# Row sums by VectorE transposes and a gate applied on the copy out of PSUM, in a fused linear-attention and FFN block

## Chip, cores and metric

The kernel runs on one core of one Trainium2 chip. The metric is device time in microseconds; the time before is the median of three runs. The profiles show one execution. Engines: PE is TensorE, DVE is VectorE, ACT is ScalarE, POOL is GpSimd, SP is the queue that issues nearly all DMAs.

## The reference

One block of a conditioned transformer, S = 2048 tokens, D = 1024, 32 heads of 32, FFN width 3584, all in bf16:

```python
mod = (silu(c) @ w_mod).reshape(1, 6, 1, -1)         # c: (1, 1024), w_mod: (1024, 6144)
sa, ca, ga, sb, cb, gb = mod[:, 0], ...
h = layernorm(x) * (1 + ca) + sa
q, k, v = heads(h @ wqkv)
phi = lambda t: where(t > 0, t + 1, exp(t)) + 1e-6
kv = einsum('bhsd,bhse->bhde', phi(k), v);  z = phi(k).sum(over s)
num = phi(q) @ kv;  den = phi(q) . z + 1e-6
x = x + ga * ((num / den) @ wo)
h = layernorm(x) * (1 + cb) + sb
x = x + gb * ((gelu(h @ w_gate) * (h @ w_up)) @ w_down)
```

## The kernel before

Every instruction is recorded by hand with what it reads and writes; semaphores follow from that. PE and SP run in the recorded order. For the stretch from the last products of k to the first output-projection products, a planner (`reorder`, with a table of costs by name) orders DVE, ACT and POOL anew by due times.

The stages, with their place in the profile: layer norm and k of the first 512 tokens (to 31 us); q and k of the rest, with phi on ACT and DVE (to 127 us); the stage that the change touches (127 to 204 us); the rest of the output projection with the second layer norm beside it (to some 250 us); the FFN's gate and up products (to 602 us); the down products (to the end).

The stage from 127 us has 24 tiles of M = phi(k)^T x, eight head groups times three column tiles (k = 0, 1, 2), each of 16 matmuls (`m_tile`, L934) into PSUM banks 0 to 3 in turn. ACT copies each to SBUF (`mb`, L939). When a group's three tiles are there, a DMA transpose on SP brings M into the form `mtb` (`m_t`). Tiles 0 to 11 are groups 0 to 3, tiles 12 to 15 the first tiles of groups 4 to 7, and 16 to 23 the other two of each. A table `HOOK` puts other work behind certain tiles:

- `kv`: `kv_prod` multiplies the transposed M of a group with the weights of v (L952, bank 4); DVE masks the diagonal blocks into `kvt` (L956).
- `w`: `w2_pair` multiplies `kvt` with the group's rows of wo (L1235, banks 6 and 7); ACT copies the pair to `W2` (L1237). Before, wo has been multiplied by the gate ga ahead of that by eight DVE instructions (`wofold`, L1241).
- `den`: phi(q) times z for half of the tokens (L1262, 32 matmuls); DVE adds 1e-6, takes the reciprocal and casts it to `RDH` (L1267 to L1269), and a DMA stores it to DRAM. `rb` loads it back spread over partitions, and `pq_scale` (L1296) multiplies phi(q) by it. z comes from `z32` (L1229), which needs a column of each group's first tile.
- `ga`, `modp`, `gbr`: the modulation rows that are needed along the free axis (ga, then sb and cb, then gb).

Those rows are eight pieces of 512 columns. DVE accumulates each over the eight row blocks of w_mod (`macc`, L855, L858, L833, L835), one 128x512 instruction at a time, so 128 partial sums per column are left. To add them, ACT writes a bf16 part (`mhi`, L864, L842) and DVE the rest (`mlo`, L868, L843), and `mod_rows` multiplies both by a matrix of ones on PE (L879). ACT copies the result out (L886), SP stores it to the DRAM row `scr_row`, and loads bring it back: `gab` and `gbb` spread over all partitions, `sbT` and `cbT` as columns.

Afterwards `wo_mm` (L1304) multiplies the scaled phi(q) with `W2`, and DVE adds the result to x (L1313, L1317). The first three chunks of tokens are interleaved with the last W2 pairs.

Of the kernel before, what the change touches and what calls it, by code (L numbers as in the profile page):

```python
# [7 lines left out]
ACTF = mybir.ActivationFunctionType  # L8
ALU = mybir.AluOpType

P = 128
# [8 lines left out]
HPG = 4  # L20
# [169 lines left out]
class Sched:  # L190
# [41 lines left out]
    def dma(self, stream, fn, rd=(), wr=(), deps=(), note="", overwrite_ok=False):  # L232
# [6 lines left out]
        if prev is not None:  # L239
# [12 lines left out]
               "nm": (0.074, 0.085), "hmod": (0.25, 0.085), "macc": (0.66, 0.085), "mlo": (0.6, 0.085), "kvt": (0.21, 0.085), "z": (0.34, 0.085),  # L252
               "dene": (0.335, 0.085), "rden": (1.67, 0.085), "pqs": (0.62, 0.085), "wofold": (1.13, 0.085), "x": (1.14, 0.085), "ssum": (1.15, 0.085), "tsum": (1.15, 0.085), "padd": (0.62, 0.085), "yT": (0.62, 0.085)},
# [96 lines left out]
def bass_adaLN_cond__linear_attn_block__geglu_ffn__prompt_kernel(  # L350
# [18 lines left out]
    with ExitStack() as es:  # L369
# [53 lines left out]
        MROW = [at(f"mrow{i}", [P, 512], f32, OFF_ROW + i * 2048) for i in range(2)]  # L423
        MROW0 = at("mrowa", [P, 256], f32, XHO[2])
        WMG = [at(f"wmg{i}", [P, 4, 512], bf16, HBO[3] + i * 4096) for i in range(2)]
        MRG = at("mrg", [P, 256], f32, OFF_TMP + 4096)
        HLG = at("hlg", [P, 2, 2, 512], bf16, OFF_TMP)
        GAC = at("gacc", [P, 512], f32, OFF_TMP + 4096)
        ACC = [at(f"acc{i}", [P, 512], f32, OFF_ROW + i * 2048) for i in range(2)]
        HLO = OFF_WS + 16384  # L430
        HL = at("hl", [P, 4, 2, 512], bf16, HLO)
# [7 lines left out]
        for name, shape, dty, sz in [  # L439
            ("ident", [P, P], bf16, 256), ("bmask", [P, P], bf16, 256), ("bm32", [P, NG, NH], bf16, 512),   # L440
            ("z32", [P, NG, NH], bf16, 512), ("rdc", [P, SGW // 2], f32, 1024), ("rdh", [P, SGW // 2], bf16, 512),
            ("ones", [P, 32], bf16, 64), ("silf", [P, NDC], f32, 64),
            ("c8", [NDC, P], bf16, 256), ("cT", [P, NDC], f32, 64), ("chalf", [P, NDC], f32, 64),
            ("thc", [P, NDC], f32, 64), ("siluT", [P, NDC], bf16, 64), ("modt", [P, 16], f32, 64), ("add4", [P, 4], f32, 64),
            ("sbT", [P, NDC], f32, 64), ("cb1T", [P, NDC], f32, 64),
            ("cbT", [P, NDC], f32, 64), ("zcols", [P, NG], f32, 64), ("neghalf", [P, 1], f32, 64),
            ("st", [P, NCH, 12], f32, NCH * 48), ("mv", [P, NCH, 2], f32, NCH * 8),
            ("rs", [P, NCH], f32, 64), ("nm", [P, NCH], f32, 64), ("ve", [P, NCH], f32, 64),
        ]:
# [7 lines left out]
        ONES, SILF, C8, CT, CHALF, THC, SILUT = (_small[k] for k in ("ones", "silf", "c8", "cT", "chalf", "thc", "siluT"))  # L457
# [78 lines left out]

        def r_hl(k, h0, h1):
            return [(HLO + (2 * (k % 4) + h0) * 1024, HLO + (2 * (k % 4) + h1) * 1024, "hl")]

# [130 lines left out]
        sch.op(V, lambda e: e.memset(ONES[:, :], 1.0), wr=r_sm("ones"))  # L670
# [155 lines left out]
        def r_hlg(j, h):  # L826
            return [(OFF_TMP + (2 * j + h) * 1024, OFF_TMP + (2 * j + h + 1) * 1024, "hlg")]

# [11 lines left out]
        def gb_hilo(j):  # L840
            acc, rng = GA_[j]
            sch.op(A, lambda e: e.activation(HLG[:, j, 0, :], acc[:, :], ACTF.Copy), rd=rng, wr=r_hlg(j, 0), note=f"mhi{6 + j}")  # L842
            sch.op(V, lambda e: e.tensor_tensor(HLG[:, j, 1, :], acc[:, :], HLG[:, j, 0, :], ALU.subtract), rd=rng + r_hlg(j, 0), wr=r_hlg(j, 1), note=f"mlo{6 + j}")  # L843

        o_gb = [None]

        def gb_rows():
            mod_rows(((0, 2, 5, lambda j, h: (HLG[:, j, h, :], r_hlg(j, h))),))
            o_gb[0] = mod_store(2, 5, MRG, [(OFF_TMP + 4096, OFF_TMP + 5120, "mrg")], 2)

# [11 lines left out]
        def mod_hi(k):  # L862
            rng = r_2k(OFF_ROW + k % 2 * 2048, f"acc{k % 2}")
            sch.op(A, lambda e: e.activation(HL[:, k % 4, 0, :], ACC[k % 2][:, :], ACTF.Copy), rd=rng, wr=r_hl(k, 0, 1), note=f"mhi{k}")  # L864

        def mod_lo(k):
            rng = r_2k(OFF_ROW + k % 2 * 2048, f"acc{k % 2}")
            sch.op(V, lambda e: e.tensor_tensor(HL[:, k % 4, 1, :], ACC[k % 2][:, :], HL[:, k % 4, 0, :], ALU.subtract),  # L868
                   rd=rng + r_hl(k, 0, 1), wr=r_hl(k, 1, 2), note=f"mlo{k}")

        def mod_rows(parts):
            for k0, n, bank, src in parts:
                o = None
                w = n * P
                for h in range(2):
                    for j in range(4):
                        ap, rng = src(k0 + j * n // 4, h)
                        ap = ap[:, j * w % 512:j * w % 512 + w]
                        o = sch.op(T, lambda e, h=h, j=j, ap=ap, bank=bank, w=w: e.matmul(  # L879
                            ps_all[32 * j:32 * (j + 1), bank * 512:bank * 512 + w], ONES[:, :], ap, start=(h == 0), stop=(h == 1)),  # L880
                            rd=rng + r_sm("ones"), pwr=(pr(bank) if h == j == 0 else ()), note=f"modr{k0}.{h}.{j}")
                pset_writer(bank, o)

        def mod_store(n, bank, dst, rng, row):
            w = n * P
            sch.op(A, lambda e: e.activation(dst[:, 0:w], ps_all[:, bank * 512:bank * 512 + w], ACTF.Copy),  # L886
                   prd=pr(bank), wr=rng, note=f"mrow{row}")
            return sch.dma(Q, lambda e: e.dma_start(scr_row[row, 0:n, :].rearrange("a (h b) -> (a h) b", b=w), dst[0:128:32, 0:w]), rd=rng, note=f"mrow{row}.st")

        def hl_src(k, h):  # L890
            return HL[:, k % 4, h, :], r_hl(k, h, h + 1)

# [214 lines left out]
        def wofold(*kcs):  # L1107
            for kc in kcs:
                rg = r_wo(kc)
                sch.op(V, lambda e, kc=kc: e.tensor_tensor(WO[:, kc, :], WO[:, kc, :], GAB[:, :], ALU.mult),  # L1110
                       rd=rg + R_GAB, wr=rg, note=f"wofold {kc}")

        def mod_step():
            mblk[0] += 1
            for f_ in late.pop(mblk[0], ()):
                f_()
            if 48 <= mdone[0] < 64:
                j, dc = divmod(mdone[0] - 48, NDC)
                mdone[0] += 1
                gb_acc(j, dc)  # L1120
                if dc == NDC - 1:
                    gb_hilo(j)
            elif mdone[0] < 48:
                k, dc = mq[mdone[0]]
                mdone[0] += 1
                mod_acc(k, dc)
                if dc == NDC - 1:
                    late.setdefault(mblk[0] + 1, []).append(lambda k=k: mod_hi(k))
                    late.setdefault(mblk[0] + 2, []).append(lambda k=k: mod_lo(k))
# [102 lines left out]
        def w2_pair(g, b0=6):  # L1232
            for half in range(2):
# [3 lines left out]
            sch.op(A, lambda e: e.activation(W2[:, g, :], ps_all[:, b0 * 512:(b0 + 2) * 512], ACTF.Copy),  # L1237
                   prd=pr(b0) + pr(b0 + 1), wr=r_w(OFF_WK, "w2", g), note=f"w2cp{g}")

        def wofold(kc):  # L1240
            sch.op(V, lambda e: e.tensor_tensor(WO[:, kc, :], WO[:, kc, :], GAB[:, :], ALU.mult), rd=r_wo(kc) + R_GAB, wr=r_wo(kc), note=f"wofold {kc}")  # L1241
# [5 lines left out]
        def mod_pass():  # L1247
            assert mdone[0] >= 48 and not late
            mod_rows(((2, 4, 5, hl_src),))
            o_r = mod_store(4, 5, MROW[1], r_2k(OFF_ROW + 2048, "mrow1"), 1)  # L1250
            for dst, nt, a0 in ((SBT, "sbT", 0), (CBT, "cbT", 2)):
                sch.dma(Q, lambda e, dst=dst, a0=a0: e.dma_start(dst[:, :], scr_row[1, a0:a0 + 2, :].rearrange("a (b p) -> p (a b)", p=P)),
                        wr=r_sm(nt), deps=[o_r], note=nt)
# [45 lines left out]
        def wo_mm(c_, b0, gs):  # L1299
# [9 lines left out]
            if gs[-1] == NG - 1:  # L1309
# [13 lines left out]
        HOOK = {0: "ga", 6: "kv0", 8: "w0", 9: "kv1", 11: "w1", 12: "kv2", 14: "w2 modp", 15: "kv3 z32", 16: "den0", 17: "w3", 18: "rb0.0",  # L1323
                19: "kv4 den1", 20: "w4 rb0.1", 21: "gbr", 22: "kv5", 23: ""}
        st = {}

        def hook_run(f):
# [4 lines left out]
            elif f == "gbr":  # L1332
                assert mdone[0] == 64
                gb_rows()
            elif f == "modp":
                mod_pass()
            elif f == "z32":
                z32()
            elif f[:3] == "den":
# [8 lines left out]
        for n, (g, k) in enumerate(tiles):  # L1348
# [5 lines left out]
            if 2 <= n <= 9:  # L1354
                wofold(n - 2)
# [13 lines left out]
        wo_mm(1, 2, E6)  # L1369
# [4 lines left out]
        wo_mm(2, 4, E6[:4])  # L1374
        w2_pair(7)
        wo_mm(2, 4, E6[4:])
# [713 lines left out]
```

## Time and profile before

| | |
|---|---|
| runs | 784.59, 785.09, 783.88 us; median 784.59 |
| profiled execution, its own time | 784.2 us |
| its span | 782.4 us |
| busy share of the span | PE 99%, DVE 83%, ACT 45%, POOL 6% |
| granted TensorE clock | 1.00 |
| DMA | 125.93 MB, mean 161 GB/s |

The profiled execution's span leaves out 1.8 us of its own time, and its time is 0.4 us below the median. A busy engine in the page is one with an instruction in flight; matmuls overlap, so the times between their starts tell more than their lengths. A row of the order of time has start, length, engine, line, operation, tiles and count; in brackets stand the idle time before it and what ended that.

### The profile page before, as it was taken

Reading aid. Unit: us, or ns where it says so; the run is one execution under the profiler, and the core shown is the slowest. Engines: PE = TensorE matmul, PEld = TensorE weight load, DVE = VectorE, ACT = ScalarE, POOL = GpSimd, SP = SyncE. Lnnn points to the kernel's source line nnn. Section 1 sums busy time; section 2 is a strip of 40 time slices with the busy share of each in tenths; the row PEclk is TensorE's granted clock in tenths of the full one; section 3 lists DMA queues with packets and bytes.
Section 4 is the critical chain, followed back from the end, with each engine's and each line's share of the span. In section 5 each row is a group of like instructions: output and inputs, shape, how many; then the busy total and the mean of one; then the engine's idle time right before and its main releaser. Section 6 shows DMA issues by size and latency. Waiting matters only on the chain.

```text
span 782.4 us, 11038 instructions
## 1 busy us (share of the span) xinstructions
PE 771.6 (99%) x3812; PEld 501.1 (64%) x3875; DVE 646.0 (83%) x1089; ACT 353.0 (45%) x585; POOL 47.4 (6%) x126
## 2 busy tenths in 40 slices
PE   8999999999999999999999999999999999999998
PEld 4444445666445677767676777767676576677766
DVE  6699989993498978897999989898889897676777
ACT  2497743333474576776554444444544111111111
POOL 2031300000230011110000000000000000000000
PEclk9999999999999999999999999999999999999999
DMA  9889749836597068747445465646545445344341
GB/s 277 261 168 251 156 96 253 222 70 115 133 257 189 28 188 255 210 127 182 125 125 162 135 197 194 194 118 199 148 121 149 155 129 160 121 142 130 120 134 41
DMA packets 210543, 125.93 MB, mean 161 GB/s; under 512 B 70444, under 2 KB 200116, under 8 KB 210488
## 3 DMA queue, kind: packets, MB, share of 16 engines
q1 hardware_dynamic: 210328, 125.16, 58.4%
q8 instruction: 31, 0.51, 0.3%
q14 instruction: 24, 0.20, 0.1%
q10 hardware_dynamic: 160, 0.07, 0.0%
HBM read 88.35 MB, written 23.22 MB: 143 GB/s over the span
## 4 chain that ended last, share of the span: by engine, by line
PE 94%; DMA 2%; SPq 2%; issue 1%; DVE 0%; ACT 0%; DVEq 0%
PE ps_all L1475 45%; PE ps_all L1688 23%; PE ps_all L970 7%; PE ps_all L1304 7%; PE ps_all L934 6%; PE ps_all L919 6%; DMA mtb<-mb 1%; SPq L632 1%; DMA wmq<-in_w_mod_dram 1%; SPq L637 1%; PE ps_all L952 0%; PE ps_all L1235 0%; PE ps_all L1262 0%; SPq L626 0%; DVE xall L1317 0%
## 5 line engine op out<-in xcount | busy, mean ns | idle before, releaser
L1475 PE MATMUL ps_all<-ss,tp 128*128 128x512 f32 x896 | 214.7, 396 | 0.0
L1475 PEld LDWEIGHTS ps_all<-ss,tp 128*128 128x128 f32 x896 | 168.1, 188 | 38.2 <-DVE ps_all L1487 0.6
L1688 PE MATMUL ps_all<-bt,xs 128*128 128x512 f32 (+1 forms) x532 | 125.6, 393 | 0.1
L1688 PEld LDWEIGHTS ps_all<-bt,xs 128*128 128x128 f32 x532 | 98.9, 188 | 22.6 <-issue 0.5
L1487 DVE TENSOR_TENSOR ps_all<-ps_all,es 128x512 f32<-128x512 f32 x112 | 77.6, 696 | 38.4 <-PE ps_all L1475 35.8
L1492 ACT ACTIVATE ge<-ps_all 128x512 f32<-128x512 f32 x112 | 64.0, 597 | 89.1 <-DVE ps_all L1487 45.0
L1496 DVE TENSOR_TENSOR yr<-ge,ps_all 128x512 bf16<-128x512 f32 x112 | 74.0, 679 | 2.2 <-PE ps_all L1475 1.6
L1443 DVE TENSOR_TENSOR tp<-wt 128x512 fp32r<-128x512 bf16 x112 | 74.1, 683 | 1.1 <-DMA wt<-in_B_w_gate_dram 0.7
L1443 DVE TENSOR_TENSOR tp<-wt,tp 128x512 fp32r<-128x512 bf16 x112 | 74.0, 682 | 0.0
L970 PE MATMUL ps_all<-h1T,wq 128*128 128x512 bf16 x256 | 56.7, 379 | 0.0
L919 PE MATMUL ps_all<-wk,h1T 128*128 128x512 bf16 x239 | 55.3, 379 | 1.1 <-DMA wk<-in_A_wqkv_dram 0.5
L1304 PE MATMUL ps_all<-w,pq 128*128 128x512 bf16 x251 | 55.9, 379 | 0.4
L1688 PE MATMUL ps_all<-bx,yl 128*128 128x512 bf16 x225 | 55.2, 380 | 0.7
L1475 PE MATMUL ps_all<-ar,tp 128*128 128x512 f32 x224 | 55.3, 389 | 0.0
L908 ACT ACTIVATE eb<-ps_all 128x512 f32<-128x512 f32 x64 | 36.4, 593 | 37.5 <-PE ps_all L919 15.5
L1475 PE MATMUL ps_all<-h20a,wt 128*128 128x512 bf16 x210 | 48.0, 379 | 0.9
L1475 PE MATMUL ps_all<-h21a,wt 128*128 128x512 bf16 x210 | 47.8, 379 | 1.0
L1475 PEld LDWEIGHTS ps_all<-ar,tp 128*128 128x128 f32 x224 | 42.0, 188 | 8.7
L1484 ACT ACTIVATE es<-ps_all 128x512 f32<-128x512 f32 x56 | 33.4, 599 | 30.8 <-PE ps_all L1475 30.8
L1481 ACT ACTIVATE ps_all<-ps_all 128x512 f32<-128x512 f32 x56 | 32.6, 582 | 31.2 <-PE ps_all L1475 30.9
L970 PEld LDWEIGHTS ps_all<-h1T,wq 128*128 128x128 bf16 x256 | 25.0, 98 | 29.9
L1304 PEld LDWEIGHTS ps_all<-w,pq 128*128 128x128 bf16 x256 | 24.7, 98 | 30.3 <-issue 0.5
(152 smaller groups left out, 889.9 us busy)
## 6 DMA issues: line engine op xcount, KB each, us to landing
wt<-in_B_w_gate_dram SPq DMA_DIRECT2D x28, 512.0 KB, 4.0
wt<-in_B_w_up_dram SPq DMA_DIRECT2D x28, 512.0 KB, 5.4
scr_y<-yr SPq DMA_DIRECT2D x56, 256.0 KB, 4.8
yl<-scr_y SPq DMA_DIRECT2D x8, 896.0 KB, 4.7
yl<-scr_y SPq DMA_DIRECT2D x14, 448.0 KB, 4.4
wmst<-in_w_mod_dram SPq DMA_DIRECT2D x6, 1024.0 KB, 5.5
wmq<-in_w_mod_dram SPq DMA_DIRECT2D x8, 512.0 KB, 6.0
rb<-scr_rd SPq DMA_DIRECT2D x32, 128.0 KB, 2.9
```

Of the source, the lines that this page charges most:

```text
L908: sch.op(A, lambda e: e.activation(EB[i][:, :], PS(bank), ACTF.Exp), prd=pr(bank), wr=rng, note=f"{note}.exp")
L919: o = sch.op(T, lambda e, dc=dc: e.matmul(PS(bank), H1[sg][:, ci, dc, :], W_[:, dc, jg * 512:(jg + 1) * 512], start=(dc == 0), stop=(dc == ...
L934: o = sch.op(T, lambda e, c_=c_: e.matmul(PS(bank, 0, n), PK[c_][:, g * P:(g + 1) * P], xrow(c_, o_, o_ + n), start=(c_ == 0), stop=(c_ == ...
L970: o = sch.op(T, lambda e, dc=dc: e.matmul(PS(b), WQ[:, dc, qc * P:(qc + 1) * P], H1[sg][:, :, dc, :], start=(dc == 0), stop=(dc == NDC - 1 ...
L1304: last[half] = sch.op(T, lambda e, g=g, half=half: e.matmul(PS(b0 + half), PQ[sg][:, g, ci * P:(ci + 1) * P], W2[:, g, half * 512:(half + ...
L1443: sch.op(V, lambda e, t=t: e.tensor_tensor(TP[k][:, t, :, :], in0[:, t, :, :], in1[:, t, :, :], ALU.subtract), rd=r0[t:t + 1] + (r1[t:t + ...
L1475: o = sch.op(T, lambda e, l_=l_, r_=r_, dc=dc: e.matmul(PS(b), l_, r_, start=fresh and dc == 0, stop=dc == ND2 - 1, skip_group_check=True) ...
L1484: sch.op(A, lambda e: e.activation(ES[t][:, :], PS(be + t), ACTF.Copy), prd=pr(be + t), wr=r_2k(OFF_ES[t], f"es{t}"), note="escp")
L1487: sch.op(V, lambda e: e.tensor_tensor(PS(dst + t), PS(BB + t), ES[t][:, :], ALU.add), prd=pr(BB + t), rd=r_2k(OFF_ES[t], f"es{t}"), pwr=pr ...
L1492: sch.op(A, lambda e: e.activation(GE[i][:, :], PS(b), ACTF.Gelu_apprx_tanh), prd=pr(b), wr=r_2k(OFF_GE[i], f"ge{i}"), note="gelu")
L1496: sch.op(V, lambda e: e.tensor_tensor(YR[:, 2 * (v % 2) + l, h * SGW:(h + 1) * SGW], GE[i][:, :], PS(b + 1), ALU.mult), rd=r_2k(OFF_GE[i], ...
L1688: pend_ = sch.op(T, lambda e, l_=l_, r_=r_, i=i: e.matmul(PS(b, c0, c1), l_, r_, start=fresh and i == 0, stop=i == n - 1, skip_group_check ...
```

## The change

1. The sums over the 128 partitions no longer go through PE. For each piece DVE transposes the accumulator in 32x32 blocks (`mtr`, 128x512) and reduces each block's row (`mred`, to 16 numbers per partition). When a row's two pieces are there, `mod_row` gathers the four groups of 32 partitions side by side (four `qcp`), adds them (`qred`), transposes 32x32 (`qtr`), and SP stores the 32x32 result to the DRAM row. The splitting into two bf16 parts on ACT and DVE, the 24 ones-matmuls and ACT's copies go. The two rows sb and cb now have a store each where they had one together.
2. wo stays as it is. DVE instead of ACT copies each W2 pair out of PSUM and multiplies it by the gate there (`wtwo`).
3. den1 follows den0 directly behind tile 16, in bank 4 where den0 has bank 5. The first run's store moves from tile 16 to tile 17, behind the transpose of M group 4, and is recorded behind den1, which casts into the same tile `RDH`.
4. kv1 moves from tile 9 to tile 10, and the first output-projection products are regrouped around the last W2 pairs.

```diff
+        def part_sum(k):
+            acc, rng = GA_[k - 6] if k >= 6 else (ACC[k % 2], r_2k(OFF_ROW + k % 2 * 2048, f"acc{k % 2}"))
+            i = k % 2
+            rt = r_2k(TRO[i], f"tr{i}")
+            sch.op(V, lambda e: e.transpose(TR[i][:, :], acc[:, :]), rd=rng, wr=rt, note=f"mtr{k}")
+            sch.op(V, lambda e: e.tensor_reduce(RDV[:, k // 2, i * 16:i * 16 + 16], TR[i][:, :].rearrange("p (a b) -> p a b", b=32), mybir.AxisListType.X, ALU.add),
+                   rd=rt, wr=r_rd(k), note=f"mred{k}")
+
+        def mod_row(v, row, a0):
+            rq, rr, rt = ([(o_, o_ + w, n)] for o_, w, n in ((QSO, 512, "qs"), (QRO, 128, "qr"), (QTO, 128, "qt")))
+            for q in range(HPG):
+                sch.op(V, lambda e, q=q: e.tensor_copy(QS[0:32, q, :], RDV[32 * q:32 * (q + 1), v, :]), ...)
+            sch.op(V, lambda e: e.tensor_reduce(QR[0:32, :], QS[0:32, :, :].rearrange("p q a -> p a q"), mybir.AxisListType.X, ALU.add), ...)
+            sch.op(V, lambda e: e.transpose(QT[0:32, :], QR[0:32, :]), rd=rr, wr=rt, note=f"qtr{v}")
+            return lambda: sch.dma(Q, lambda e: e.dma_start(scr_row[row, a0:a0 + 2, :].rearrange("a (h i) -> (a h) i", i=32), QT[0:32, :]), rd=rt, note=f"mrow{v}.st")
...
         def ga_pass():
-            b = 6
-            mod_rows(((0, 2, b, hl_src),))
-            o_r = mod_store(2, b, MROW0, [(XHO[2], XHO[2] + 1024, "mrow0")], 0)
-            row_load(GAB, R_GAB, 0, 0, "gab", o_r)
+            row_load(GAB, R_GAB, 0, 0, "gab", mod_row(0, 0, 0)())
...
-            sch.op(A, lambda e: e.activation(W2[:, g, :], ps_all[:, b0 * 512:(b0 + 2) * 512], ACTF.Copy),
-                   prd=pr(b0) + pr(b0 + 1), wr=r_w(OFF_WK, "w2", g), note=f"w2cp{g}")
-
-        def wofold(kc):
-            sch.op(V, lambda e: e.tensor_tensor(WO[:, kc, :], WO[:, kc, :], GAB[:, :], ALU.mult), rd=r_wo(kc) + R_GAB, wr=r_wo(kc), note=f"wofold {kc}")
+            sch.op(V, lambda e: e.tensor_tensor(W2[:, g, :], ps_all[:, b0 * 512:(b0 + 2) * 512], GAB[:, :], ALU.mult),
+                   prd=pr(b0) + pr(b0 + 1), rd=R_GAB, wr=r_w(OFF_WK, "w2", g), note=f"wtwo{g}")
...
         def mod_pass():
             assert mdone[0] >= 48 and not late
-            mod_rows(((2, 4, 5, hl_src),))
-            o_r = mod_store(4, 5, MROW[1], r_2k(OFF_ROW + 2048, "mrow1"), 1)
+            o_r = [mod_row(v, 1, 2 * v - 2)() for v in (1, 2)]
...
-        HOOK = {0: "ga", 6: "kv0", 8: "w0", 9: "kv1", 11: "w1", 12: "kv2", 14: "w2 modp", 15: "kv3 z32", 16: "den0", 17: "w3", 18: "rb0.0",
-                19: "kv4 den1", 20: "w4 rb0.1", 21: "gbr", 22: "kv5", 23: ""}
+        HOOK = {0: "ga", 6: "kv0", 8: "w0", 10: "kv1", 11: "w1", 12: "kv2", 14: "w2 modp", 15: "kv3 z32", 16: "den0 den1", 17: "st0 w3", 18: "rb0.0",
+                19: "kv4", 20: "w4 rb0.1", 21: "gbr", 22: "kv5", 23: ""}
...
-                st[int(f[3:])] = den(int(f[3:]), 5)
-                if f == "den0":
-                    st[0]()
+                st[int(f[3:])] = den(int(f[3:]), 5 - int(f[3:]))
...
-            if 2 <= n <= 9:
-                wofold(n - 2)
...
         wo_mm(0, 0, E6)
         kv_prod(6, 4)
-        wo_mm(1, 2, E6)
+        wo_mm(1, 2, E6[:4])
         kv_prod(7, 5)
         w2_pair(6)
         rb_load(1)
         x_dma(NXR, 10)
-        wo_mm(2, 4, E6[:4])
+        wo_mm(1, 2, E6[4:])
+        wo_mm(2, 4, E6[:3])
         w2_pair(7)
-        wo_mm(2, 4, E6[4:])
+        wo_mm(2, 4, E6[3:])
```

More of the change, by code (lines that the diff above doesn't have):

```diff
@@ L441, in bass_adaLN_cond__linear_attn_block__geglu_ffn__prompt_kernel @@
             ("z32", [P, NG, NH], bf16, 512), ("rdc", [P, SGW // 2], f32, 1024), ("rdh", [P, SGW // 2], bf16, 512),
-            ("ones", [P, 32], bf16, 64), ("silf", [P, NDC], f32, 64),
+            ("silf", [P, NDC], f32, 64),
             ("c8", [NDC, P], bf16, 256), ("cT", [P, NDC], f32, 64), ("chalf", [P, NDC], f32, 64),
@@ L871, in mod_rows @@
[L871 to L891, printed above, removed]
+        def r_rd(k, n=1):
+            return [(RDO + k * 64, RDO + (k + n) * 64, "rdv")]
@@ L1121, in mod_step @@
                 if dc == NDC - 1:
[L1122 removed]
+                    part_sum(6 + j)
             elif mdone[0] < 48:
```

54 lines of the change are left out of this document (17 added, 37 removed).

## The prediction

> **What bounds the kernel now.** I read the page first, then the matmul engine's order of time from 126 to 262 us (where everything the diff touches is issued), then VectorE's busy time by stretch, its groups and its order of time, and last the DMA queue SP, because the edits move stores there.
>
> ```profile
> span 782.4 us, 11038 instructions
> PE 771.6 (99%) x3812; PEld 501.1 (64%) x3875; DVE 646.0 (83%) x1089; ACT 353.0 (45%) x585; POOL 47.4 (6%) x126
> PE 94%; DMA 2%; SPq 2%; issue 1%; DVE 0%; ACT 0%; DVEq 0%
> 150.00:160.00 10.00, 9.84 (x72) 6.45 (x72) 9.82 (x17) 3.83 (x7) 0.00 (x0) 1.00 0.18 41
> 160.00:170.00 10.00, 9.95 (x82) 6.45 (x82) 9.75 (x16) 4.58 (x12) 0.00 (x0) 1.00 0.47 125
> 170.00:180.00 10.00, 9.95 (x94) 6.40 (x93) 6.60 (x11) 2.91 (x5) 0.00 (x0) 1.00 0.36 57
> ```
>
> The first three lines are of the page: TensorE (PE) is busy 99% of the span and carries 94% of the chain that ended last. The other three are stretches (start:end, length, then PE, PEld, DVE, ACT and POOL busy with counts, granted clock, DMA share, GB/s). PE never pauses there, and VectorE (DVE) is almost as full up to 170 us, at 9.8 of 10, and has air only after that. So two things count. A matmul that leaves PE is worth its full time. And DVE work that is added before 170 us has little to hide behind: PE waits as soon as something that it needs comes late out of DVE's queue, or out of SP's queue behind DVE.
>
> **The change part by part.** First what leaves PE. Rows are start, length, engine, line, operation; a tile of M is 16 matmuls, shown as 7 and 9.
>
> ```profile
> 128.41 1.47 PE L934 MATMUL ps_all<-xall,pk 128*128 128x341 bf16 x9
> 129.81 0.40 PE L879 MATMUL ps_all<-hl,ones 128*32 128x256 bf16 x8
> 130.14 1.19 PE L934 MATMUL ps_all<-xrow,pk 128*128 128x342 bf16 x7
> 131.17 1.47 PE L934 MATMUL ps_all<-xall,pk 128*128 128x342 bf16 x9
> 132.47 1.18 PE L934 MATMUL ps_all<-xrow,pk 128*128 128x342 bf16 x7
> ...
> 150.63 1.47 PE L934 MATMUL ps_all<-xall,pk 128*128 128x341 bf16 x9
> 152.21 0.62 PE L952 MATMUL ps_all<-mtb,wv 128*128 128x128 bf16 x8
> ...
> 165.37 0.38 PE L1235 MATMUL ps_all<-wo,kvt 128*128 128x512 bf16 x1
> 165.68 0.62 PE L879 MATMUL ps_all<-hl,ones 128*32 128x512 bf16 x8
> 166.22 1.19 PE L934 MATMUL ps_all<-xrow,pk 128*128 128x341 bf16 x7
> ...
> 170.02 1.47 PE L934 MATMUL ps_all<-xall,pk 128*128 128x342 bf16 x9
> 171.41 1.06 PE L1262 MATMUL ps_all<-pq,z 128*32 128x256 bf16 x32
> 172.40 1.19 PE L934 MATMUL ps_all<-xrow,pk 128*128 128x342 bf16 x7
> ...
> 174.96 0.38 PE L1235 MATMUL ps_all<-wo,kvt 128*128 128x512 bf16 x1
> 175.17 1.18 PE L934 MATMUL ps_all<-xrow,pk 128*128 128x342 bf16 x7
> ...
> 185.22 1.47 PE L934 MATMUL ps_all<-xall,pk 128*128 128x342 bf16 x9
> 186.96 1.19 PE L934 MATMUL ps_all<-xrow,pk 128*128 128x342 bf16 x7
> ```
>
> *Row sums off PE (L879).* Nine matmuls of M normally take 132.47 - 131.17 = 1.30 us. With the first group of ones-matmuls behind them it is 130.14 - 128.41 = 1.73, so the group costs 0.43. The third group: 186.96 - 185.22 - 1.30 = 0.44. The second stands behind a W2 pair, whose second matmul is followed after 175.17 - 174.96 = 0.21 where no group stands; there it is 166.22 - 165.37 = 0.85, so 0.64. Together 1.51 us, all on the path.
>
> *kv1 one tile later (hook 9 to 10).* From 150.63 to 152.21 are 1.58 us instead of 1.30: PE waits 0.28 for the transposed M of group 1. A tile later (2.3 us) that has landed: 0.28 gained. Nothing needs kv1 before the W2 pair after tile 11.
>
> *Both den runs back to back.* Going into den costs 171.41 - 170.02 - 1.30 = 0.09 us beyond the nine matmuls (another tile shape); I take the same for going out. Two runs together pay this once instead of twice: 0.18.
>
> Sum: 1.51 + 0.28 + 0.18 = 1.97 us off PE, and ScalarE loses work that nobody waited for. The regrouped output-projection matmuls (L1304) are as many as before.
>
> Now what DVE and SP must deliver for that to hold.
>
> ```profile
> L1317 DVE TENSOR_TENSOR xall<-ps_all,xall 128x1024 bf16<-128x1024 f32 x8 | 9.8, 1220 | 3.4 <-PE ps_all L1304 3.4
> L868 DVE TENSOR_TENSOR hl<-acc,hl 128x512 bf16<-128x512 f32 x6 | 4.0, 683 | 0.1
> L991 DVE BATCH_NORM_STATS2 st<-xall 128x6 f32<-128x512 bf16 x8 | 5.3, 685 | 0.9 <-DMA xall<-in_A_x_dram 0.9
> L909 DVE TENSOR_SCALAR eb<-eb 128x512 f32<-128x512 f32 x64 | 25.6, 419 | 6.3 <-ACT eb L908 6.0
> L1268 DVE RECIPROCAL rdc<-rdc 128x256 f32<-128x256 f32 x2 | 3.5, 1748 | 0.0
> L995 DVE TENSOR_SCALAR ve<-mv 128x1 f32<-128x1 f32 x4 | 0.6, 154 | 0.1
> ...
> 130.02 4.05 DVE L858 SCALAR_TENSOR_TENSOR acc<-wmst,silf,acc 128x512 f32<-128x512 bf16 x6
> 140.06 5.77 DVE L1241 TENSOR_TENSOR wo<-wo,gab 128x1024 bf16<-128x1024 bf16 x5 [0.81 <-DMA gab<-scr_row]
> 149.40 0.38 PE L1235 MATMUL ps_all<-wo,kvt 128*128 128x512 bf16 x1
> ```
>
> From start to start a DVE instruction takes less than its mean: five wofolds last 5.77 = 4 x 1.14 + 1.22, six accumulations 4.05 = 5 x 0.66 + 0.74; a 128x512 TENSOR_TENSOR 0.60. The gate now rides on the copy out of PSUM (wtwo): L1317 is that instruction form, 1.22, so eight wofolds (9.1 us) become eight wtwos (9.1 us), spread over 149 to 200 us instead of standing together at 140. The eight subtractions (L868, L843, 4.8 us) go. Added: eight transposes and eight reduces of 128x512, and four sets of six small instructions at about 0.1 to 0.15 each (L995). The trace shows no DVE transpose and no TENSOR_REDUCE. Bounds from rows: 0.34 (L909, 0.42 shown) and 3.4 (L1268, 1.75 for 256). I take 0.6: L868 streams the same 128x512, L991 reads 512 and writes 6. So DVE gains some 7 us net, and the question is where.
>
> *Up to 150 us there is room*: the 9.1 us of wofolds leave, two sets of row sums (2.4 + 0.6 each) come. DVE waits at wtwo0 for the W2 pair 0: second matmul 149.40 + 0.38, less 0.43: 149.35.
>
> *149.35 to z32*, which starts den0. In the built order stand there 21 accumulations (13.9), wtwo0 and wtwo1 (2.3), two kvt (0.5), two transposes and two reduces (2.4): 19.1, so z32 runs at 168.45 and ends by 168.9. PE reaches den0 at 171.41 - (0.43 + 0.28 + 0.64) = 170.06. Margin 1.2.
>
> *SP.* The row stores of sb and cb, the loads sbT and cbT, and the transpose of M group 4 stand in this order; the first den store moves behind that transpose. And RDH is one tile: the first store is now recorded behind the second run's cast into it, so it waits for rden1 (and carries that run's values).
>
> ```profile
> 167.74 0.54 SPq L888 DMA_DIRECT2D scr_row<-mrow  x1
> 170.81 0.37 SPq L1252 DMA_DIRECT2D sbT<-scr_row  x1
> 178.14 2.02 SPq L1283 DMA_DIRECT2D rb<-scr_rd  x4
> 180.54 1.23 SPq L735 DMA_TRANSPOSE mtb<-mb  x1
> ...
> DMA to landing us min/median/max: 3.1/3.1/3.1
> ...
> scr_rd<-rdh SPq DMA_DIRECT2D x2, 64.0 KB, 1.8
> ...
> 179.91 0.62 PE L952 MATMUL ps_all<-mtb,wv 128*128 128x128 bf16 x8
> 189.29 0.61 PE L952 MATMUL ps_all<-mtb,wv 128*128 128x128 bf16 x8
> ```
>
> (The landing line is the transpose at 180.54 alone.) After z32 DVE does six small ones, kvt3, wtwo2, an accumulation, a transpose: about 3.1, so the last row store starts at 172.0 or, if the estimates above are generous, 171.4. It lands as in the rows above after 170.81 - 167.74 = 3.1; sbT and cbT follow, the transpose of group 4 starts at 175.5 to 176.1, and 3.1 later it has landed, 178.6 to 179.2. PE reaches kv4 at 179.91 - 1.35 + 0.9 (den1 now stands ahead of it) = 179.46. Margin 0.3 to 0.9. Then wtwo3 waits for its pair (175.34 - 1.35 + 0.9 = 174.9) till 176.1; dene1, two accumulations, rden1 and the cast 3.6: 179.7, instead of the store's old 176.3. It lands after 1.8; four rb loads and the transpose of group 5 start at 181.5 and 183.9 (178.14 to 180.54 was 2.4 too), landed 187.0. PE reaches kv5 at 189.29 - 1.97 = 187.3. Margin 0.3, where it was 5.6. At the end wtwo6 and wtwo7 (1.2 each) have 10 and 8 matmuls of 0.22 to hide behind: covered by 0.3 to 0.9.
>
> All covers hold by these numbers, the last two barely. Forecast: -2.0 us. On the profiled execution's own 784.2 that is 782.2; the median of the runs lies 0.4 higher (784.59), so **782.6 us**.
>
> **The rivals.** (1) *The late transposes make kv4 or kv5 wait.* Every 0.1 us that DVE or a landing is later than worked out beyond the margin is 0.1 on PE. The landing of 3.1 is one sample; 1 us more gives a wait of 0.1 to 0.7. For it: DVE has no idle time from 149 to 179 in this order. Price 0.5 to 1.5: 783.1 to 784.1, in the main no change that can be told.
>
> The Trainium skill (VectorE: DVE Perf Modes, Two Vector instructions with no wait between them) says that an instruction starting in another group of 32 partitions waits until all earlier ones are finished. The copies that gather the four row groups do that; by that rule each would pay its whole 0.15 and not 0.1, 0.2 us a set, which eats most of the margin at kv4. No row here shows it.
>
> (2) *The transposes take two passes*, 1.2 us for 128x512. Between wtwo0 and rden1 stand three: 3 x 0.6 = 1.8 later, less a margin of 0.3: waits of 1.5 at kv4 and kv5, a gain of 0.5: 784.1.
>
> By the Trainium skill (the same page, The three transpose paths) a 128x128 bf16 transpose on VectorE takes 311 ns; four of those are an estimate of 1.24, which is this rival. But four short instructions pay any fixed start four times; I stay with 0.6.
>
> (3) *Slower: DVE becomes the bound ahead of den0, kv4 and kv5.* If a transpose or reduce costs c, five of them stand between wtwo0 and the last row store, so the waits are 5 x (c - 0.6) - 0.3. They eat the 1.97 at c = 1.05 and make it slower by 0.2% at c = 1.37. At c = 1.5 they are 4.2, a loss of 2.2: 786.8, and more where kvt and the W2 pairs come late too. For it: the row sums sit where DVE is at 9.8 of 10, and nothing in the trace prices them. Against it: every 512-wide DVE row quoted here is at 0.75 or less.
>
> (4) *The gain does not reach the end*: after 222 us DVE is busy for long and PE is tied to it. Before the FFN's first products it still stops for PE now and then, so this has a small chance, at 784.5.
>
> **How the numbers follow.** Forecast 0.53, rival 1 0.17, rival 2 0.08, rival 3 0.20, rival 4 0.02. The measurement of this kernel tells about 0.2% (1.6 us, below 783.0) from no change. The forecast lies only 0.4 inside that, so I count nine tenths of it as faster, and a third of rival 1: 0.54. Rivals 2 and 4 and the rest of these are same: 0.26. Rival 3 is slower: 0.20. Range: 781.9 (the forecast with kv4's old wait and the runs' scatter of 0.6) to 785.6, which takes in rivals 1, 2 and 4 and the milder third of rival 3.
>
> **What would show it.** Right: PE rows from tile to tile without L879, 1.30 per nine; kv1 no wait; wo starts near 190.5 instead of 192.5; transposes and reduces near 0.7 each. Wrong: PE idle in front of den0, kv4 or kv5, released by DVE or by the transposes of M; rden0's store later than 181 us; transposes at over 1 us.

## The result and the profile after

The changed kernel takes 782.76 us (median of 11 runs, 781.75 to 783.33), the kernel before 784.59 beside it. The ratio is 0.9973, with a 95% interval of 0.9965 to 0.9982: faster by 0.27%. A second group of runs gave 0.9965 (0.9952 to 0.9978). The forecast was 782.6. The profiled execution's span is 780.6 us, 1.8 less than before; its own time is 783.07, so 2.5 us lie around the span where 1.8 did before.

First the page of the changed kernel (span, busy time, the chain that ended last), and then the three stretches of the stage that the prediction showed.

```profile
span 780.6 us, 11063 instructions
PE 773.8 (99%) x3851; PEld 501.2 (64%) x3851; DVE 654.2 (84%) x1120; ACT 339.9 (44%) x566; POOL 46.8 (6%) x126
PE 96%; SPq 2%; DMA 1%; DVE 0%; issue 0%
```

```profile
150.00:160.00 10.00, 10.00 (x80) 6.87 (x78) 9.89 (x16) 2.06 (x6) 0.00 (x0) 1.00 0.18 41
160.00:170.00 10.00, 10.00 (x78) 6.57 (x79) 9.88 (x22) 1.56 (x7) 0.00 (x0) 1.00 0.49 133
170.00:180.00 10.00, 10.00 (x125) 7.09 (x118) 10.00 (x16) 1.81 (x4) 0.00 (x0) 1.00 0.26 29
```

From 150 to 180 us VectorE (DVE) is now full: 10.00 of 10 in the last of these stretches, where it had 6.60. PE does not pause in them. Just ahead of them DVE has got room. These are the ten microseconds from 140 us, first before and then after the change:

```profile
140.00:150.00 10.00, 9.95 (x74) 6.72 (x73) 9.94 (x11) 2.09 (x7) 0.00 (x0) 1.00 1.26 320
```

```profile
140.00:150.00 10.00, 10.00 (x75) 6.73 (x73) 5.73 (x15) 1.89 (x5) 0.00 (x0) 1.00 1.27 317
```

DVE was busy for 9.94 of 10 there and is busy for 5.73 now. Next PE's order of time in the changed kernel (start, length, line, operation, count).

```profile
128.25 1.47 PE L907 MATMUL ps_all<-xall,pk 128*128 128x341 bf16 x9
129.56 1.18 PE L907 MATMUL ps_all<-xrow,pk 128*128 128x342 bf16 x7
...
152.35 1.47 PE L907 MATMUL ps_all<-xall,pk 128*128 128x342 bf16 x9
153.65 0.61 PE L925 MATMUL ps_all<-mtb,wv 128*128 128x128 bf16 x8
...
168.48 1.47 PE L907 MATMUL ps_all<-xall,pk 128*128 128x342 bf16 x9
169.88 1.93 PE L1221 MATMUL ps_all<-pq,z 128*32 128x256 bf16 x64
171.74 1.19 PE L907 MATMUL ps_all<-xrow,pk 128*128 128x342 bf16 x7
...
179.16 0.61 PE L925 MATMUL ps_all<-mtb,wv 128*128 128x128 bf16 x8
...
185.70 1.47 PE L907 MATMUL ps_all<-xall,pk 128*128 128x342 bf16 x9
187.26 0.62 PE L925 MATMUL ps_all<-mtb,wv 128*128 128x128 bf16 x8
...
190.47 2.75 PE L1263 MATMUL ps_all<-w,pq 128*128 128x512 bf16 x12
```

The ones-matmuls are gone: behind the nine matmuls that end the first tile the next tile starts after 129.56 - 128.25 = 1.31. kv1 starts 1.30 after its tile (153.65 - 152.35): no wait. Both den runs stand together in 171.74 - 169.88 = 1.86. The output projection starts at 190.47 instead of 192.50. One new wait is there: kv5 starts 187.26 - 185.70 = 1.56 after its tile, 0.26 late. The chain that ended last, in order of time, names what it waited for:

```profile
183.61 3.60 DMA mtb<-mb
...
187.26 0.62 PE ps_all L925 x8
```

The chain leaves PE for the transpose of M group 5, issued at 183.61 and landed at 187.21.

How far the stage got shorter is read best as one distance, because the start of the kernel differs by some tenths from execution to execution: from the first matmul of the first tile of M to the first output-projection product of the fourth chunk of tokens. It was 77.28 us before and is 75.36 now, 1.92 less; the second profile of the same kernel gives 1.98.

### The profile page after: what moved, and what is told of

Its sections match the earlier page's. It is cut to its first block, busy times and chain, and to the rows that moved or that the text cites. A ratio compares the mean times of both kernels' runs of the same rounds, so it can differ in the third digit from the quotient of the medians.

```text
span 780.6 us, 11063 instructions
## 1 busy us (share of the span) xinstructions
PE 773.8 (99%) x3851; PEld 501.2 (64%) x3851; DVE 654.2 (84%) x1120; ACT 339.9 (44%) x566; POOL 46.8 (6%) x126
## 4 chain that ended last, share of the span: by engine, by line
PE 96%; SPq 2%; DMA 1%; DVE 0%; issue 0%
PE ps_all L1433 45%; PE ps_all L1646 23%; PE ps_all L1263 7%; PE ps_all L943 7%; PE ps_all L907 7%; PE ps_all L892 6%; SPq L630 1%; DMA wmq<-in_w_mod_dram 1%; SPq L635 1%; PE ps_all L925 0%; DMA mtb<-mb 0%; PE ps_all L1198 0%; SPq L624 0%; PE ps_all L1221 0%; DVE ps_all L1688 0%
## 5 line engine op out<-in xcount | busy, mean ns | idle before, releaser
L1433 PE MATMUL ps_all<-h21a,wt 128*128 128x512 bf16 x224 | 51.0, 380 | 0.0
L1433 PE MATMUL ps_all<-h20a,wt 128*128 128x512 bf16 x224 | 50.9, 380 | 0.0
L1263 PEld LDWEIGHTS ps_all<-w,pq 128*128 128x128 bf16 x256 | 24.8, 98 | 30.1 <-issue 0.5
```

The source lines that it names most:

```text
L1263: last[half] = sch.op(T, lambda e, g=g, half=half: e.matmul(PS(b0 + half), PQ[sg][:, g, ci * P:(ci + 1) * P], W2[:, g, half * 512:(half + ...
L1433: o = sch.op(T, lambda e, l_=l_, r_=r_, dc=dc: e.matmul(PS(b), l_, r_, start=fresh and dc == 0, stop=dc == ND2 - 1, skip_group_check=True) ...
```

## The experiments

The change has three parts that can be set apart: the row sums on DVE (rows), the gate on the copy out of PSUM (gate), and the new places of kv1, the den runs and the first store (order). All eight combinations were run. The regrouped output-projection products were not set apart: the four kernels with the row sums on DVE have them, the four without do not. "Stage" is the change of the distance above, in each kernel's profile; the ratio is of all runs to the kernel before on the same chip.

| kernel | rows | gate | order | stage, us | ratio (95%) |
|---|---|---|---|---|---|
| before | | | | 0 | 1 |
| order_only | | | x | -0.61 | 0.9995 (0.9986 to 1.0004) |
| gate_only | | x | | +0.75 | 1.0001 (0.9991 to 1.001) |
| gate_order | | x | x | -0.46 | 0.9995 (0.9986 to 1.0005) |
| rows_only | x | | | +2.32 | 1.0026 (1.0017 to 1.0035) |
| rows_order | x | | x | +0.98 | 1.0023 (1.0013 to 1.0034) |
| rows_gate | x | x | | +0.93 | 1.0011 (1.0002 to 1.002) |
| the change | x | x | x | -1.92, -1.98 | 0.9973 (0.9965 to 0.9982) |

The stage is read from one execution, the ratio from all. For rows_order the two differ: five of its eight runs had a granted clock of 0.997 or 0.998 and took 786.67 to 787.31, while the three at 1.000, the profiled one among them, took 785.19, 785.39 and 786.02, which is 0.7 to 1.5 above the 784.51 of before and fits the 0.98. What lowered the clock is open.

My theory was that the 1.51 us of ones-matmuls come out only because other parts make room on DVE and give the transposes of M time to land; the rival, that the parts add up.

**The row sums alone.** The kernel before with `part_sum` and `mod_row`, and with the regrouped output-projection products.

```diff
-        def mod_rows(...):        # bf16 parts, ones-matmuls on PE
+        def part_sum(k): ...      # transpose, reduce
+        def mod_row(v, row, a0): ...
         HOOK, wofold, w2_pair     # as before
```

> The kernel before with the row sums by VectorE transposes alone: the gate still on wo ahead, den runs and kv1 where they were. Theory (PE gives up 1.51 us, but the eight wofolds stand together on DVE from 142 us and push what follows): kv1 waits 0.6 more (PE gets there earlier, the transpose does not), the W2 pair 1 waits for kvt1 behind the wofolds for 1 to 1.8 us, kv4 for its transpose for 1 to 1.6: no gain, 0.5 to 2.4 us slower than the kernel before. Rival (matmuls off PE are worth their time, DVE has room): 1.2 to 1.5 us faster.

786.96 us, ratio 1.0026: slower, by 2.0 us. These are PE's waits in the stage, grouped (engine, line, who was waited for: us, times, longest), and the DVE rows behind them. L925 is kv1 and kv4, L1198 the W2 pair 1; all three waits were expected, and in about these sizes.

```profile
PE ps_all L925 <- DMA mtb<-mb: 2.0, 2, 1.3
PE ps_all L1198 <- DVE kvt L929: 1.8, 1, 1.8
```

```profile
142.85 5.71 DVE L1204 TENSOR_TENSOR wo<-wo,gab 128x1024 bf16<-128x1024 bf16 x5
148.49 0.27 DVE L929 TENSOR_TENSOR kvt<-ps_all,bmask 128x128 bf16<-128x128 f32 x1
148.69 2.34 DVE L1204 TENSOR_TENSOR wo<-wo,gab 128x1024 bf16<-128x1024 bf16 x2
...
158.80 0.70 DVE L854 STREAM_TRANSPOSE tr<-acc 128x512 f32<-128x512 f32 x1
159.43 0.25 DVE L929 TENSOR_TENSOR kvt<-ps_all,bmask 128x128 bf16<-128x128 f32 x1
```

The row sums of ga delay the wofolds from 140.06 to 142.85; everything behind them follows, until the second masked product is ready only at 159.7 (159.43 + 0.25), and W2 pair 1 has waited 1.8 for it. So DVE does become the bound when the row sums come without the gate.

**The gate alone.**

```diff
-            sch.op(A, lambda e: e.activation(W2[:, g, :], ps_all[...], ACTF.Copy), ...)
+            sch.op(V, lambda e: e.tensor_tensor(W2[:, g, :], ps_all[...], GAB[:, :], ALU.mult), ...)
-            if 2 <= n <= 9:
-                wofold(n - 2)
```

> The kernel before with the gate on the copy out of PSUM alone. Theory (as many microseconds on DVE, only later; nothing leaves PE): within 0.3 us of the kernel before; kv4's wait of 0.09 may go, the last W2 copy (1.22 on DVE for 1.02 on ACT) may make the output projection wait 0.2. Rival (ACT's copies and the wofolds were in somebody's way): faster by 0.5 or more.

785.0 us, ratio 1.0001: no change, as far as the time tells. In its profile kv1 waits 0.82 for the transpose of M (L952, DMA mtb<-mb), which was not expected, and the stage is 0.75 longer. This need not be the gate: the transpose of M group 1 was issued 15.2 us after the first tile of M, 0.1 later than in the kernel before, but landed at 25.5 instead of 24.8, and in the twelve profiles that landing lies anywhere between 24.5 and 25.8. The gate by itself gains nothing.

**The order alone, and the order left out.**

```diff
-        HOOK = {..., 9: "kv1", ..., 16: "den0", 17: "w3", 18: "rb0.0", 19: "kv4 den1", ...}
+        HOOK = {..., 10: "kv1", ..., 16: "den0 den1", 17: "st0 w3", 18: "rb0.0", 19: "kv4", ...}
```

> The kernel before with the new order alone: kv1 behind tile 10, both den runs behind tile 16, the first den store behind the transpose of M group 4 and behind the second run's cast. Row sums stay on PE and wo is still multiplied by the gate. The prediction's terms for this are 0.28 (the wait at kv1) and 0.18 (one shape switch less): about -0.45 us, 784.1, too little to tell by time; in the trace kv1 without a wait, one run of 64 den matmuls, no new wait, the distance from the first tile of M to the first output-projection product of chunk 3 shorter by 0.4 to 0.6. Rival: the later first den store makes kv5 wait here too; the margin before was 5.6 us and the store goes some 3.4 later, so none is expected. If waits at kv4 or kv5 appear, the order by itself costs what the prediction put down to DVE.

The stage is 0.61 shorter, with no wait; the time (783.97, ratio 0.9995) can't tell it from before. The later first den store cost nothing here. This is PE's row for the two runs together in this kernel:

```profile
170.90 1.93 PE L1262 MATMUL ps_all<-pq,z 128*32 128x256 bf16 x64
```

> The changed kernel with the order of before: kv1 behind tile 9, den0 and den1 apart, the first store directly behind den0. Row sums on DVE and the gate on the copy stay. If the parts add up, this is -1.51 us, 783.1. My theory after the two single parts: they do not add up. PE reaches kv1 a tile earlier (2.3 us) with M group 1 transposed no earlier, so it waits 0.5 to 1.0 there, and 0.5 to 1.2 again at kv4, where den1's matmuls no longer stand ahead as cover: 783.9 to 784.9, no change that can be told. Then the moves are worth far more than the 0.46 of their own terms, because they are the cover of the rest.

With rows and gate but the old order, it is 785.24 us, ratio 1.0011, 0.3 us above the theory's range, and the stage is 0.93 longer. The waits grouped in its stage, and the two rows that wait:

```profile
PE ps_all L925 <- DMA mtb<-mb: 2.5, 2, 1.3
```

```profile
152.26 0.62 PE L925 MATMUL ps_all<-mtb,wv 128*128 128x128 bf16 x8 [1.32 <-DMA mtb<-mb]
...
180.61 0.62 PE L925 MATMUL ps_all<-mtb,wv 128*128 128x128 bf16 x8 [1.23 <-DMA mtb<-mb]
```

kv1 and kv4 wait where the theory put the waits, 1.32 and 1.23 where 0.5 to 1.0 and 0.5 to 1.2 were expected. Moving kv1 a tile later and the second den run ahead of kv4 is what hides both; their own terms in the prediction were 0.46, and leaving them out costs 2.85 (0.93 + 1.92). Up to 0.6 of that can be scatter: the transpose that kv1 waits for landed 25.5 us after the first tile of M here, and at 24.9 in rows_only and in the changed kernel.

**The gate left out, and the row sums left out.** The same patches: rows and order with wofolds (rows_order), gate and order with ones-matmuls (gate_order).

```diff
 rows_order:   part_sum, mod_row, new HOOK;  wofold and w2_pair as before
 gate_order:   wtwo, new HOOK;               mod_rows with ones-matmuls as before
```

> The changed kernel without the gate on the copy: row sums on DVE and the new order, wo still multiplied by the gate in eight DVE instructions. The row sums alone lost 0.88 at kv1, 1.92 at W2 pair 1 and 1.44 at kv4. Theory: the eight instructions standing together are what the row sums collide with, and the order cannot heal that: the wait at kv1 goes, but W2 pair 1 waits for a masked product that DVE finishes no earlier, so it waits longer by as much, and at kv4 the second den run covers 0.9: 785.6 to 786.8, slower than before. Rival: once kv1 stands a tile later everything finds room and the parts add up (-1.51 - 0.46): 782.6, and the gate's part of the change is worth nothing.

> The changed kernel without the row sums on DVE: ones-matmuls on PE as before, the gate on the copy out of PSUM, and the new order. The gate alone moved nothing (785.0), with a wait of 0.98 at kv1 and 0.19 at a W2 copy. Theory: with kv1 a tile later that wait goes, and what is left is the order's 0.46 to 0.61: 784.0 to 784.4, nothing that the time can tell; the gate gives no time by itself, it only makes room on DVE. Rival: moving the copies from ACT to DVE costs at the last W2 pairs and in front of kv5, which now waits for a later store: 784.8 or more.

rows_order takes 786.72 us, ratio 1.0023: slower, as the theory had it, and the rival (782.6) is out, also by the three runs at a clock of 1.000 (785.19 and more). Its waits in the stage:

```profile
PE ps_all L1198 <- DVE kvt L929: 2.8, 2, 2.5
PE ps_all L925 <- DMA mtb<-mb: 0.3, 1, 0.3
```

The wait at kv1 is gone and W2 pair 1 waits 2.5 instead of 1.8, so the same collision on DVE is paid one step later. gate_order takes 784.1 us, ratio 0.9995, and no matmul waits at kv1 to kv5; but a weight load (PEld) in the output projection waits for the gated copy of W2 pair 6:

```profile
PEld ps_all L1301 <- DVE w L1237: 0.5, 1, 0.5
```

PE loses 0.19 by it: the seventh product behind the last W2 pair starts 0.40 after the sixth instead of 0.22. gate_only has the same pause, the kernel before one of 0.05, and no kernel with the regrouped products has one at that place. So the gate with the order gains no more than the order. With the gate and the order in place, the row sums and the regrouping together are worth 1.46 us (-1.92 against -0.46), of which 0.19 is this pause; without either the gate or the order the row sums cost.

**Each transpose twice.** This puts the price of rival 2 into the kernel.

```diff
-            sch.op(V, lambda e: e.transpose(TR[i][:, :], acc[:, :]), rd=rng, wr=rt, note=f"mtr{k}")
+            for _ in range(2):
+                sch.op(V, lambda e: e.transpose(TR[i][:, :], acc[:, :]), rd=rng, wr=rt, note=f"mtr{k}")
```

> The changed kernel with each 128x512 transpose done twice: the same result, eight more DVE instructions of 0.60 us start to start, which is what rival 2 of the prediction assumed. By the prediction's sum three of them stand between the first gated copy and the second den run's reciprocal: 1.8 later, less the margins that were measured at kv4 (0.24) and kv5 (0 or less): about 1.5 us of waits, 784.1 to 784.4. Rival: DVE is not full there (it waits for PE at two of the gated copies, 1.8 and some tenths), so part of the 1.8 is taken up: 0.3 to 0.8 us of waits, 783.0 to 783.5. Where the waits stand (kv3, kv4, kv5) tells which.

783.4 us, ratio 0.9985 (0.9976 to 0.9994), within the rival's 783.0 to 783.5, and the stage is 1.68 shorter than before: eight more instructions of 0.6 us cost 0.24 there, not 1.5. By PE's starts kv3 is 0.32 late and kv5 0.20, where the changed kernel had only kv5's 0.26. The order of time on DVE shows where the rest stayed.

```profile
149.41 1.23 DVE L1201 TENSOR_TENSOR w<-ps_all,gab 128x1024 bf16<-128x1024 f32 x1 [0.92 <-PE ps_all L1199]
...
180.42 0.27 DVE L1229 CAST rdh<-rdc 128x256 bf16<-128x256 f32 x1
```

The transposes of ga went into DVE's wait for the first pair (0.92 is left of 1.79). Between there and the second run's cast, the planner moved the transpose of a piece of gb, which has time, behind it, and z32 ahead of the second reduce; the cast is 0.70 later than the 179.72 of the changed kernel, not 1.8. Rival 2's sum held the order fixed, which the planner does not. The stage explains 0.24 of the 0.6 by which this kernel's median lies above the changed kernel's 782.76 (from another group of runs); its profile loses another 0.5 in the down products, which is told below.

**A tile for each den run's reciprocals.** The first store then waits for the first run alone, and carries its own values. (The edit is shortened.)

```diff
-            sch.op(V, lambda e: e.tensor_copy(RDH[:, :], RDC[:, :]), ...)
+            RDH = RDH2[pr_]           # two tiles
+            sch.op(V, lambda e: e.tensor_copy(RDH[:, :], RDC[:, :]), ...)
```

> The changed kernel once more, as the measure for the others of this group. Theory (PE bound: 1.97 us less on PE, one new wait of 0.26 in front of kv5): 1.6 to 2.0 us under the kernel before. On PE's order of time the distance from the first M tile to the first output-projection product of the fourth chunk shortens by 1.9 us, and the wait of 0.3 us that the first profile shows in the down stage is not there again if it is the run's own. Rival (the gain was made elsewhere, or part of it is luck of one execution): other distances.

> The changed kernel with a second tile for the reciprocals of the second den run (its first store carries the first run's values again). Theory (kv5 waits because the first store waits for the second run's cast at 179.9): the store starts at about 177 and not 180.1, the transpose of M group 5 at about 181 and not 183.6, kv5's wait of 0.26 us goes: 0.25 us faster than the changed kernel, 2.1 under the kernel before. Rival (the transpose lands late from traffic, whatever it starts after): kv5 still waits, no difference.

The changed kernel once more (after_again) gave 782.55 us (0.9965), 2.4 under the kernel before and more than the 1.6 to 2.0 expected; its stage is 1.98 shorter. The one with two tiles gave 782.19 (0.9963, 0.9949 to 0.9977); the times don't tell them apart. SP's order of time in the one with two tiles:

```profile
177.26 0.52 SPq L1233 DMA_DIRECT2D scr_rd<-rdh  x1
179.26 1.82 SPq L1245 DMA_DIRECT2D rb<-scr_rd  x4
181.19 1.24 SPq L734 DMA_TRANSPOSE mtb<-mb  x1
```

The store starts 2.8 us earlier than in the changed kernel (180.06) and the transpose of group 5 2.4 earlier; kv5 does not wait, and the stage is 2.19 shorter than before instead of 1.92. So the wait at kv5 comes from the store behind the second run's cast. It is a matter of tenths: in the second profile of the changed kernel the transpose lands 0.07 ahead of kv5's start, and PE loses 0.20 a little later, in the first chunk of the output projection.

The second tile matters for another reason. In the changed kernel, and in every kernel here with the new order and one tile, the first store goes out after the second run's cast into that tile (179.72, store at 180.06). It carries the second run's reciprocals, so the first half of the tokens is divided by the denominators of the other half. That is an error of the new order. Only the two kernels with two tiles are free of it, and as they are not slower, the gain does not come from it.

**The down products.** Behind the stage the whole gain was carried unchanged for over 400 us, and then part of it was lost at one place: at 635.6 PE waits for an addition on DVE (L1688). In the profile of two tiles the loss was 0.67, in that of the changed kernel 0.30. DVE's chain to that addition begins with the sum that needs the last piece of y. Its rows in the changed kernel, in its second profile, and with two tiles:

```profile
625.64 0.96 DVE L1640 TENSOR_TENSOR xs<-yl,yl 128x768 fp32r<-128x768 bf16 x1 [3.15 <-DMA x1s<-scr_x]
```

```profile
625.71 0.96 DVE L1640 TENSOR_TENSOR xs<-yl,yl 128x768 fp32r<-128x768 bf16 x1 [2.66 <-DMA yl<-scr_y]
```

```profile
625.71 0.96 DVE L1643 TENSOR_TENSOR xs<-yl,yl 128x768 fp32r<-128x768 bf16 x1 [3.25 <-DMA x1s<-scr_x]
```

Set against PE's first product of the second token group, this sum starts 2.99, 2.77 and 3.31 us later; it was 2.66 before. What PE then loses is 0.30, 0.09 and 0.67, and nothing before: the excess over 2.66, to 0.03. The order alone (3.13, 0.48) and the doubled transposes (3.21, 0.53) stand on the same line. So DVE's chain has no slack there, and what is given back is the lateness of one landing. Two executions of the same kernel differ by 0.22 in it, so a part of the lateness is scatter. But in the five kernels whose stage is longer than before, or shorter by less than 0.5, the sum starts 2.67 to 2.74 late, and in the six that are 0.6 or more shorter it starts 2.55 to 3.31 late. So the landing may not follow a PE that comes earlier; that is not shown, and why it varies is open.

The last experiment has two tiles and gives that chain slack.

```diff
-            if j == 1:
-                devac(0, 1)          # two DVE instructions for an output tile
             dprod(j, 6, 0, NST)
             dpadd(j, BC)             # the addition that PE waits for
+            if j == 1:
+                devac(0, 1)
```

> The changed kernel with a tile of its own for each den run's reciprocals (so that the first store does not wait for the second run and carries its own values), and in the down stage one more exchange on DVE: the addition that PE waits for at 635.65 is issued ahead of the two instructions that finish an output tile, 1.3 us earlier. Theory: the shift of 2.34 us that the profile with the second tile had until 599 is given back there because the DVE chain behind the last y load has no slack; with 1.3 us of slack it reaches the end: span 780.0 to 780.2, 781.5 to 781.8, ratio about 0.996. Rival: the time is given back at the next place where DVE and PE meet, and it stays at 782.2; or the exchange delays an output store that something waits for.

Its profiled span is 780.2 us, the shortest of all profiles, PE loses nothing in the down products and the shift of 2.18 reaches the end. But the landing came early in this execution (2.55), so that the old order would have lost nothing either, and the time, 782.16 us (0.9971, 0.9958 to 0.9983) where 781.5 to 781.8 was expected, can't be told from that of two tiles or of the change. That this exchange is worth anything is not shown.

## Why the prediction was right

The forecast's sum and its order of events came out nearly as written.

*What leaves PE.* The ones-matmuls 1.51 and kv1's 0.28 are gone in full. The two den runs together take 1.86, and 0.10 to go in (169.88 - 168.48 - 1.30); before, each took 172.40 - 171.41 = 0.99 and 0.09 to go in. The gain is 2.16 - 1.96 = 0.20, where 0.18 stood. kv4's old wait of 0.09 went as well, which the prediction had only in the low end of its range; kv5 waits 0.26. That is 1.82 of the 1.92 measured. Another 0.05 is the pause in the output projection that the regrouping ends; the rest is too small to place. The order alone gave 0.61 for the terms of 0.28, 0.18 and 0.09.

*DVE's prices.* They are in the groups of the changed kernel (busy time and mean ns behind the bar).

```profile
L1200 DVE TENSOR_TENSOR w<-ps_all,gab 128x1024 bf16<-128x1024 f32 x8 | 9.7, 1215 | 3.3 <-PE ps_all L1198 3.2
L855 DVE TENSOR_REDUCE rdv<-tr 128x16 f32<-128x512 f32 x8 | 5.1, 660 | 0.0
L854 DVE STREAM_TRANSPOSE tr<-acc 128x512 f32<-128x512 f32 x7 | 4.7, 689 | 0.0
L861 DVE COPY qs<-rdv 32x32 f32<-32x32 f32 x16 | 2.7, 169 | 0.4
L862 DVE TENSOR_REDUCE qr<-qs 32x32 f32<-32x128 f32 x4 | 1.4, 352 | 0.0
L863 DVE STREAM_TRANSPOSE qt<-qr 32x32 f32<-32x32 f32 x4 | 0.7, 186 | 0.1
```

Transposes (689 ns) and reduces (660 ns) are the "near 0.7 each" that it asked for, the gated copy 1.215 the 1.22 of L1317. Rivals 2 and 3 needed 1.2 and more than 1.05: neither holds, by the row alone. The small ones were mis-sized: a set of six takes 1.2 us, not 0.6.

*The walk from z32 to kv5.* These are DVE's rows and then SP's, of the changed kernel.

```profile
168.11 0.41 DVE L1192 TENSOR_TENSOR z<-bm,zcols 128x256 bf16<-128x256 bf16 x1
168.44 0.77 DVE L861 COPY qs<-rdv 32x32 f32<-32x32 f32 x4
169.24 0.29 DVE L929 TENSOR_TENSOR kvt<-ps_all,bmask 128x128 bf16<-128x128 f32 x1
...
171.87 0.16 DVE L863 STREAM_TRANSPOSE qt<-qr 32x32 f32<-32x32 f32 x1
...
179.72 0.27 DVE L1228 CAST rdh<-rdc 128x256 bf16<-128x256 f32 x1
```

```profile
166.90 5.48 SPq L864 DMA_DIRECT2D scr_row<-qt  x2
...
175.89 1.25 SPq L732 DMA_TRANSPOSE mtb<-mb  x1
180.06 0.34 SPq L1230 DMA_DIRECT2D scr_rd<-rdh  x1
181.69 1.82 SPq L1242 DMA_DIRECT2D rb<-scr_rd  x4
183.61 1.24 SPq L732 DMA_TRANSPOSE mtb<-mb  x1
```

z32 was put at 168.45 and ran at 168.11; the 0.6 by which the small ones were too cheap came back out of that, and the last row's result is ready at 172.03, where 172.0 stood. The transpose of group 4 starts at 175.89 (175.5 to 176.1) and lands 3.0 later, at 178.9 (178.6 to 179.2), 0.24 ahead of kv4. The first store starts at 180.06 (179.7), the transpose of group 5 at 183.61 (183.9). It landed at 187.21 (187.0): the one sample of a landing, 3.1, was too short, and it took 3.60, although four rb loads stand ahead of both. PE was there at 187.00 (187.3), 0.16 of it because this execution reached the first tile of M earlier. So the margin of 0.3 became a wait of 0.26. That is rival 1 at a quarter of a microsecond, below the 0.5 to 1.5 that it was priced at, and PE idle in front of kv5 is one of the signs that the prediction named against itself.

*Right for the stated reason.* "Up to 150 us there is room", because the wofolds leave, was the sentence that everything hung on. From 140 to 150 us DVE's busy time did fall from 9.94 to 5.73 of 10. rows_only and rows_order show it from the other side: with the wofolds in place the same row sums make the stage 2.32 and 0.98 longer, which is rival 3's end by another cause, a full queue and not a high price. That the new order is cover and not only 0.46 of gain was in the walk (den1 standing ahead of kv4), but not said as a price; rows_gate puts it at 2.85.

*Luck.* That the median came within 0.2 us of the forecast is in part luck. From the first tile of M to the start of the last matmul the first profile is 1.61 shorter than that of the kernel before (650.52 against 652.13) and the second 1.87, where the sum had 1.97: what was lost behind it, at kv5 or in the first output-projection products and in the down products, was not in the sum.

*Not foreseen.* Rival 4 had the gain lost behind 222 us, where PE is tied to DVE. It is lost in part, but only in the down products, by 0.09 to 0.67, and by a landing.

The Trainium skill (VectorE: DVE Perf Modes, Two Vector instructions with no wait between them) had the four gathering copies each wait for the one before. The trace agrees: four copies of 169 ns take 169.24 - 168.44 = 0.80, 0.20 each and longer than themselves, while the 128x512 instructions beside them start 0.6 apart at 0.69 long. The prediction, with 0.15 a copy, made this 0.2 more per set; it is 0.4 more, 0.80 where four times 0.1 stood.

The Trainium skill (the same page, The three transpose paths) led to an estimate of 1.24 for a 128x512 transpose, as four times its 311 ns. The trace has 0.689 for one instruction of that width, in fp32 where the page has bf16, so four times the figure is too much here.

## What to carry to other kernels

When work moves onto an engine that is already full, ask what leaves that engine in the same stretch: here the row sums pay only because eight multiplications leave the queue ahead of them, and the same edit without that is slower. Walk the moved work through the engine's queue and the DMA queue behind it to the next operand that the bounding engine needs; that way the walk found both places where it got tight, but a margin of 0.3 us came out as 0.24 at kv4 and as a wait of 0.26 at kv5, so such a margin is none. When a store moves behind a later write of the tile that it reads, ask which values it carries. And try the parts in all combinations: alone, no part of this change gains anything that the time can tell, one loses, and only the three together (with the regrouping) win.

## What the hardware showed beyond that

One sample of a DMA landing is not a bound. The transpose of M group 5 took 3.1 us from issue to landing in the kernel before, and 3.60 and 3.31 in two executions of the changed kernel, each time behind four loads of 128 KB. That of group 4 took 3.04 and 3.05 in the two executions of the changed kernel, with only two 4 KB loads issued just before it, and that of group 1 took 9.4 to 10.4 in the twelve profiles. The row stores of 4 KB behind 160 us in the changed kernel took 3.3, 2.7 and 4.1 us, about as long as the transposes.

A reduce of 32x128 strided numbers to 32x32 took 352 ns, a 32x32 copy 169 ns.
